# Loading K and Q of two head pairs in one transfer each instead of two

## The chip, the cores and the metric

The kernel runs on one core of a Trainium2 chip. The core has a tensor engine (PE, with its weight loads shown apart as PEld), a vector engine (DVE), a scalar engine (ACT), a general engine (POOL, GpSimd) and a sync engine (SP) that here only starts transfers. Transfers between the chip's memory and the core's on-chip memory are moved by 16 DMA engines that SP, ACT and POOL feed through queues of their own.

The metric is the device time of one execution in microseconds (us); the lower the better. The time before is a median of four runs.

## The reference

Attention over 4 batches, 8 heads, 768 positions and a head size of 64, then a feed-forward layer with a maximum of three products. Some heads ("retrieval") see all earlier positions, the others only the first 4 positions and a window of 64.

```python
scores = (1.0 / np.sqrt(D)) * np.matmul(q, k.transpose(0, 1, 3, 2))
rel = pos[:, None] - pos[None, :]
causal = rel >= 0
stream_keep = causal & ((pos[None, :] < n_sink) | ((rel >= 0) & (rel < window)))
mask = np.where(retr[:, None, None], causal, stream_keep)      # per head
scores = np.where(mask, scores, -1e9)
a = np.exp(scores - max); a = a / (sum(a) + 1e-09)
x = np.matmul(a, v)  ->  (B * S, H * D)                        # 3072 x 512
h = np.maximum(np.maximum(x @ w1, x @ w2), x @ w3)             # 3072 x 768
out = h @ w_out                                                # 3072 x 512
```

## The kernel before

Each batch is cut into two halves of 384 query positions. The unit of attention is a pair of heads (hp 0 to 3), or a group of four heads (a "quad", two pairs). Each pair goes through scores on PE (line 441), exponentials on ACT (line 452), masks, and the product with V on PE (line 495). The feed-forward layer of a half (`ffn`, lines 319 to 373) is cut into small steps that are put between the attention of the next halves, so that PE always has something to do. The order of all work is written out by hand: first a list of calls (lines 539 to 594) for the first half, then a table (lines 602 to 650). Every engine executes its instructions in that order; there is no scheduler that moves them.

The first batch loads K and Q in another way than the later ones. `load_pairs` (line 121) takes a half, the first pair, the number of pairs n and two engines, and starts the transfers of K (on SP for the first half) and of Q (on ACT for the first half) into a staging tile. With its last argument `alone` it starts one transfer per pair; without it, one for all n pairs. Rows of 768 bytes (3 positions of 64 numbers of 4 bytes) are moved. For the first half the calls are: pair 0 (line 213), the flags `ir32` that say which head is of which kind (line 215), pair 1 (line 216), pairs 2 and 3 with `alone` (line 217), and V of the first half in three transfers on SP (`load_v`, line 218). For the second half of the first batch the transfers of pairs 0 and 1 (line 563) and of pairs 2 and 3 (line 579) are started by POOL, one each for K and Q, without `alone`.

Then `cast_pair` (line 135) turns K and Q of a pair into 16-bit numbers: pair 0 on ACT, pair 1's K on POOL and Q on ACT, pairs 2 and 3 on POOL. `turn_pair` (line 147) transposes them on PE (line 157) and copies the result to the tile KQ on DVE (line 162). The order of the calls around this is: cast pair 0; ten matmuls of idle work on PE; flags; turn pair 0; cast pair 1; turn pair 1; cast pair 2; scores of pairs 0 and 1; start of the transfer of w0 on POOL (`load_weight`, line 307); `far_flags` (DVE, and two copies on POOL, line 290); cast pair 3; turn pair 2; scores of pair 1; turn pair 3; the preparation of V (`prep_v`, lines 392 and 394); scores of pairs 2 and 3; products with V. On POOL, casts, starts of transfers and copies stand in one row in this order.

The completion of each transfer that SP or ACT start is told by one of eight semaphores, taken in turn. A transfer that is the ninth to use one waits, on the engine that starts it, until the first has landed. The staging tile of pairs 2 and 3 is one tile for both in either case.

Of the kernel before, what the change touches and what calls it, by code (L numbers as in the profile page):

```python
# [51 lines left out]
def kernel(  # L52
# [14 lines left out]
    nc = tc.nc  # L67
# [53 lines left out]
    def load_pairs(half, hp, n, engines, alone=False):  # L121
        for nm, src, eng in zip(("ks", "qs"), (k, q), engines):
            st = stage.tile([P, 4, HB, D], FP32, tag=nm, name=nm)
            m = 2 if alone else 2 * n
            for h in range(0, 2 * n, m):
                eng.dma_start(
                    out=st[:, h : h + m],
                    in_=src[
                        0, 2 * hp + h : 2 * hp + h + m, half * HALF : (half + 1) * HALF
                    ].rearrange("h (p j) d -> p h j d", p=P),  # L130
                )
            for i in range(n):
                staged.setdefault((half, hp + i), []).append(st[:, 2 * i : 2 * i + 2])
# [69 lines left out]
    def load_v(b, half, engines=None):  # L203
        engines = engines or (nc.sync,) * HB
        vs = stage.tile([P, H, HB, D], FP32, tag="vs", name="vs")
        for j in range(HB):
            r0 = half * HALF + j * P
            engines[j].dma_start(
                out=vs[:, :, j], in_=v[b, :, r0 : r0 + P].rearrange("h p d -> p h d")
            )  # L210
        staged_v[b, half] = vs
# [2 lines left out]
    ir32 = consts.tile([1, 2 * H], mybir.dt.int32, name="ir32")  # L214
    nc.sync.dma_start(out=ir32, in_=is_retrieval.bitcast(mybir.dt.int32).unsqueeze(0))
    load_pairs(0, 1, 1, (nc.sync, nc.scalar))
    load_pairs(0, 2, 2, (nc.sync, nc.scalar), True)
    load_v(0, 0)


# [506 lines left out]
```

## Time and profile before

| what | value |
|---|---|
| median of four runs | 202.36 us (202.06 to 202.9) |
| profiled execution, its time | 202.53 us |
| profiled execution, its span | 200.6 us |
| PE busy | 189.1 us, 94% of the span |
| ACT busy | 131.8 us, 66% |
| DVE busy | 123.7 us, 62% |
| POOL busy | 122.4 us, 61% |
| share of DMA in the chain that ended last | 3% |
| transfers of ks on SP (first half), each | 192 KB, 4 of them |
| transfers of qs on ACT (first half), each | 192 KB, 4 of them |
| transfers of vs on SP, each | 256 KB |

The span goes from the first to the last instruction; the execution's time has 1.9 us more. A timeline row has the start in us, the length, the engine, the line, the operation with output and input, and in brackets how long the engine was idle before and what ended that. The chain that ended last is found by following back from the last instruction what each one waited for. A row of the view of stretches has the stretch, its length, busy time and instructions of PE, PEld, DVE, ACT and POOL, the granted clock of PE, the mean share of the DMA engines and GB/s. The time of a transfer to landing counts from the start of its issue.

### The profile page before, as it was taken

Reading aid. Unit: us, or ns where it says so; the run is one execution under the profiler, and the core shown is the slowest. Engines: PE = TensorE matmul, PEld = TensorE weight load, DVE = VectorE, ACT = ScalarE, POOL = GpSimd, SP = SyncE. Lnnn points to the kernel's source line nnn. Section 1 sums busy time; section 2 is a strip of 40 time slices with the busy share of each in tenths; the row PEclk is TensorE's granted clock in tenths of the full one; section 3 lists DMA queues with packets and bytes.
Section 4 is the critical chain, followed back from the end, with each engine's and each line's share of the span. In section 5 each row is a group of like instructions: output and inputs, shape, how many; then the busy total and the mean of one; then the engine's idle time right before and its main releaser. Section 6 shows DMA issues by size and latency. Waiting matters only on the chain.

```text
span 200.6 us, 5133 instructions
## 1 busy us (share of the span) xinstructions
PE 189.1 (94%) x2059; PEld 109.1 (54%) x2059; DVE 123.7 (62%) x242; ACT 131.8 (66%) x206; POOL 122.4 (61%) x153
## 2 busy tenths in 40 slices
PE   7697999796899999999999999999999999999992
PEld 2355654355566466574655465575655555755652
DVE  2699697999777738871554739961555234443540
ACT  4488698597885777666788595757768769313221
POOL 3499159579987914887969726699937537500000
PEclk9789999999999999999999999999999999999999
DMA  5999999997629993714449998602401220023004
GB/s 182 266 174 276 276 236 211 212 228 178 169 42 165 158 235 133 157 23 116 123 79 147 143 261 139 109 20 75 144 20 23 104 76 20 3 51 147 3 0 157
DMA packets 43245, 26.48 MB, mean 132 GB/s; under 512 B 33558, under 2 KB 38230, under 8 KB 43222
## 3 DMA queue, kind: packets, MB, share of 16 engines
q1 hardware_dynamic: 37206, 15.01, 34.6%
q0 software_dynamic: 4784, 10.23, 26.2%
q10 hardware_dynamic: 1232, 0.92, 1.5%
q8 instruction: 16, 0.26, 0.6%
q14 instruction: 7, 0.06, 0.1%
HBM read 25.17 MB, written 6.29 MB: 157 GB/s over the span
## 4 chain that ended last, share of the span: by engine, by line
PE 82%; ACT 5%; DVE 5%; DMA 3%; issue 2%; SPq 0%; POOL 0%; DVEq 0%; ACTq 0%
PE yy L338 42%; PE yy L364 13%; PE st L441 11%; PE oacc L495 9%; ACT pt L452 3%; PE yst L338 3%; DMA ks<-in_k_dram 2%; DVE KQ L190 2%; PE tr L157 1%; PE st L425 1%; DVE x L505 1%; DMA out_dram<-ot 1%; PE yst L364 1%; ACT va L392 1%; ACT ot L370 1%
## 5 line engine op out<-in xcount | busy, mean ns | idle before, releaser
L479 POOL TENSOR_TENSOR pt<-pt,mk 128x512 f16<-128x512 f16 (+1 forms) x76 | 80.4, 1081 | 37.6 <-ACT pt L452 37.6
L452 ACT ACTIVATE pt<-st 128x1024 f16<-128x1024 f32 (+3 forms) x99 | 83.1, 894 | 22.5 <-PE st L441 21.8
L349 DVE TENSOR_TENSOR acc<-yy,acc 128x384 f16<-128x384 f32 x45 | 25.1, 558 | 27.8 <-PE yy L338 18.4
L338 PE MATMUL yy<-xT,w2t 128*128 128x384 f16 x180 | 35.9, 327 | 1.7 <-DVE hT L349 1.7
L338 PE MATMUL yy<-xT,w1t 128*128 128x384 f16 x180 | 36.1, 327 | 0.1
L338 PE MATMUL yy<-xT,w0t 128*128 128x384 f16 x180 | 35.6, 326 | 0.2 <-DVE xT L531 0.2
L346 ACT CAST acc<-yy 128x384 f16<-128x384 f32 x45 | 21.3, 484 | 17.6 <-PE yy L338 11.2
L364 PE MATMUL yy<-woutt,hT 128*128 128x512 f16 (+1 forms) x138 | 32.0, 375 | 0.0
L441 PE MATMUL st<-KQ 32*128 32x384 f16 (+4 forms) x560 | 29.0, 281 | 0.6 <-DVE KQ L190 0.5
L349 DVE TENSOR_TENSOR hT<-yy,acc 128x384 f16<-128x384 f32 x45 | 24.9, 559 | 6.7 <-PE yy L338 4.3
L495 PEld LDWEIGHTS <-pt 128*128 128x128 f16 x672 | 23.9, 97 | 5.4 <-issue 2.2
L338 PEld LDWEIGHTS <-w2t 128*128 128x128 f16 x192 | 17.6, 98 | 15.2 <-issue 4.0
L190 DVE STREAM_TRANSPOSE KQ<-kq 128x384 f32<-128x384 f32 x24 | 25.7, 1131 | 0.0
L338 PEld LDWEIGHTS <-w0t 128*128 128x128 f16 x192 | 18.2, 98 | 12.7 <-issue 0.8
L495 PE MATMUL oacc<-va,pt 128*128 128x65 f16 x352 | 24.8, 193 | 0.3 <-ACT va L392 0.3
L338 PEld LDWEIGHTS <-w1t 128*128 128x128 f16 x192 | 17.3, 98 | 12.5 <-issue 1.3
L370 ACT COPY ot<-yy 128x512 f32<-128x512 f32 x22 | 12.9, 588 | 15.5 <-PE yy L364 9.3
L495 PE MATMUL oacc<-vf,pt 128*128 128x65 f16 x320 | 21.1, 193 | 0.9 <-POOL vf L394 0.9
L364 PEld LDWEIGHTS <-hT 128*128 128x128 f16 x150 | 13.9, 98 | 14.6 <-issue 0.3
L441 PEld LDWEIGHTS <-KQ 32*128 32x128 f16 (+1 forms) x560 | 12.2, 93 | 17.7 <-issue 12.4
L505 DVE TENSOR_TENSOR x<-oacc,rc 128x384 f16<-128x384 f32 x32 | 17.8, 558 | 1.3 <-DVE rc L503 0.3
L503 DVE RECIPROCAL rc<-oacc 128x6 f32<-128x6 f32 x32 | 6.2, 192 | 20.2 <-PE oacc L495 19.8
(71 smaller groups left out, 129.5 us busy)
## 6 DMA issues: line engine op xcount, KB each, us to landing
out_dram<-ot SPq DMA_DIRECT2D x23, 256.0 KB, 3.1
vs<-in_v_dram SPq DMA_DIRECT2D x21, 256.0 KB, 6.3
kq<-in_k_dram POOLq DMA_DIRECT2D x6, 384.0 KB, 5.8
kq<-in_q_dram POOLq DMA_DIRECT2D x6, 384.0 KB, 8.1
qs<-in_q_dram ACTq DMA_DIRECT2D x4, 192.0 KB, 4.4
ks<-in_k_dram SPq DMA_DIRECT2D x4, 192.0 KB, 4.4
w0t<-in_moe_w_dram POOLq DMA_DIRECT2D x1, 768.0 KB, 7.0
ks<-in_k_dram POOLq DMA_DIRECT2D x2, 384.0 KB, 6.8
```

What stands on the lines that cost most here:

```text
L190: nc.vector.transpose(out=dst.rearrange("c (p j) -> c j p", j=n)[:, j0:j1], in_=src.rearrange("c (j i) -> c j i", i=R),)
L338: nc.tensor.matmul(yy[:, 0:HALF], w_t[wi][:, ks, ni * P : (ni + 1) * P], xT[b, half][ks].rearrange("p a t -> p (a t)"), start=(ks == 0), s ...
L346: nc.scalar.copy(out=acc[ni], in_=yy[:, 0:HALF])
L349: nc.vector.tensor_tensor(out=dst, in0=yy[:, 0:HALF], in1=acc[ni], op=ALU.max)
L364: nc.tensor.matmul(yo[:, 0:n], hT[ns][:, tb * P : (tb + 1) * P], woutt[:, ns, c : c + n], start=(ns == 0), stop=(ns == NNB - 1),)
L370: op(out=ot[:, c : c + n], in_=yo[:, 0:n])
L441: nc.tensor.matmul(sts[g // m][:, g % m, c0 : c0 + n * P], KQ[rows, 0, ki * P : (ki + 1) * P], KQ[rows, 1, t0 : t0 + n * P], start=(c0 == ...
L452: nc.scalar.activation(out=pts[t, i][:, u, h0 : h0 + m, 0:w], in_=st[:, :, 0:w], func=AF.Exp, scale=sc,)
L479: engine.tensor_tensor(out=x, in0=x, in1=m, op=ALU.mult)
L495: nc.tensor.matmul(o[:, qi, hl, 0 : D + 1], pt[:, u, hl, c : c + P], vv[:, 2 * hp + hl, ki, 0 : D + 1], start=(idx == 0), stop=(idx == len ...
L503: nc.vector.reciprocal(out=rc, in_=o[:, :, :, D])
L505: nc.vector.tensor_tensor(out=x, in0=o[:, :, :, 0:D], in1=rc.unsqueeze(3).to_broadcast([P, HB, 2, D]), op=ALU.mult,)
```

## The change

K and Q of pairs 2 and 3 of the first half are loaded by one transfer of 384 KB each, where there were two of 192 KB each. Nothing else is edited. The staging tile, the rows moved and the casts are the same; each cast of pair 2 or 3 now reads from a transfer that carries both pairs. There are two transfers fewer among those that take the eight semaphores in turn, so each later one takes a semaphore two places on. In the second half the loads were already one transfer each.

```diff
     load_pairs(0, 1, 1, (nc.sync, nc.scalar))
-    load_pairs(0, 2, 2, (nc.sync, nc.scalar), True)
+    load_pairs(0, 2, 2, (nc.sync, nc.scalar))
     load_v(0, 0)
```

## The prediction

> **What bounds the kernel now.** Read in this order: the page's busy shares, its chain of work, the order of events in the first 20 us on PoolE, the tensor engine's clock by window, and the DMA issues with their landings. PE is busy for 94% of the span and the chain belongs to it; DMA holds 3%, so a load counts only where it is on the chain.
>
> ```profile
> PE 189.1 (94%) x2059; PEld 109.1 (54%) x2059; DVE 123.7 (62%) x242; ACT 131.8 (66%) x206; POOL 122.4 (61%) x153
> PE 82%; ACT 5%; DVE 5%; DMA 3%; issue 2%; SPq 0%; POOL 0%; DVEq 0%; ACTq 0%
> ```
>
> The change is in the first microseconds, so the chain in order of time is read there. It goes from K of pair 1 (landed 6.71) over one PoolE cast to PE, and PE is without a gap from 7.32 to 13.2, where ACT's exponentials take over:
>
> ```profile
> 1.71 5.00 DMA ks<-in_k_dram
> ...
> 6.76 0.51 POOL kn L139
> ...
> 7.32 0.53 PE tr L157 x6
> ...
> 12.07 0.44 PE tr L157 x6
> 12.51 0.33 PE st L425 x4
> 12.84 0.34 PE st L441 x4
> ...
> 13.20 1.35 ACT pt L452 x3
> ```
>
> PE works strictly in order here, so a late input of the transposes at 12.07 (pair 3) holds all that follows. Those inputs come from PoolE, whose timeline is (start, length, instruction, idle before it and what ended it):
>
> ```profile
> 7.97 0.51 POOL L139 CAST kn<-ks 128x384 f16<-128x384 f32 x1 [0.70 <-DMA ks<-in_k_dram]
> 8.42 0.51 POOL L139 CAST qn<-qs 128x384 f16<-128x384 f32 x1
> 8.87 0.93 POOL L307 DMA_DIRECT2D w0t<-in_moe_w_dram  x1
> 9.99 0.71 POOL L290 COPY vf<-far 128x32 f16<-128x32 f16 x2 [0.19 <-PE st L441]
> 10.53 0.68 POOL L139 CAST kn<-ks 128x384 f16<-128x384 f32 x1
> 11.15 0.56 POOL L139 CAST qn<-qs 128x384 f16<-128x384 f32 x1
> ```
>
> PoolE waits 0.70 us for pair 2's K and after that only 0.19 us before it has cast pair 3's Q (end 11.71). The last view gives, per stretch, PE's busy time, its granted clock (third from the end of the line) and DMA:
>
> ```profile
> 4.27:7.68 3.41, 1.70 (x18) 0.97 (x17) 1.32 (x5) 1.84 (x5) 0.50 (x1) 1.00 1.10 312
> 7.68:11.10 3.42, 3.42 (x23) 1.36 (x20) 3.16 (x9) 1.57 (x3) 2.95 (x6) 0.50 1.26 194
> 14.51:17.92 3.41, 2.77 (x61) 2.19 (x59) 3.10 (x10) 2.56 (x5) 3.41 (x6) 1.00 1.09 307
> ```
>
> A stretch with PE half idle (1.70 of 3.41) is followed by one at half clock; one with 2.77 of 3.41 is not (17.92 to 21.34 ran at 1.00). DMA is saturated (share about 1) from 3 us on.
>
> Landings, issue plus time to landing: pair 0 K 4.0, Q 4.3; pair 1 Q 5.0, K 6.71 (15 of its 16 completions were in by 5.45, one came late); pair 2 Q 6.95, K 2.15+5.8 = 7.92; pair 3 Q 8.14, K 4.29+4.4 = 8.67; V 9.87, 11.01, 11.98. So transfers land nearly in the order of issue, some 0.6 us apart.
>
> [...]
>
> **The change, part by part.**
>
> 1. *Removed: two issues.* SP issues ks three times instead of four, ACT qs three instead of four. ACT saves one issue, 0.50 us (the issues at 1.34, 1.87 and 2.39 are about 0.52 apart), so its table load starts near 2.4, not 2.91, and the cast of pair 0's K can begin at its landing, 4.05, not 4.31. Gain: nothing, because PE runs its warm-up matmuls until 5.06 and transposes pair 0 at 5.10; those casts were done at 4.80 and 5.22. Without that cover it would be 0.26 us.
>
> 2. *Removed: SP's wait.* SP sat 1.7 us before the fourth ks (issued 4.29, after pair 0's Q had landed), because eight completion counters go round among transfers of SP and ACT and that one was the ninth. With two transfers fewer, the merged ks (2.15) and the first V (about 2.6) go without a wait, the second V follows at 4.29, the third at about 4.9. In the kernel before V went at 4.70, 5.22, 5.84. Earlier issue gains nothing in landings: [...] the same bytes stand in the same order in front of V. SP's next instruction after V is at 35.92, so a V issue [...] (the third took 2.48 us before) holds nobody.
>
> 3. *Added: pair 2 waits for pair 3.* Casts of pair 2's K and Q on PoolE now need the whole merged transfers. I expect Q to land between 7.0 and 8.2 and K, last, at L. The bytes up to that point are the same 1.57 MB as before, so L should be that of the old last piece, 8.67; [...] so I take 8.75. Bounds: 7.92, if it is as early as pair 2's K alone was, and 9.1, if one engine is late by as much again as the spread within ks of pair 3 (about 0.4).
>
> 4. *What PoolE does with it.* Cast K at L+0.05, cast Q 0.45 later, issue of w0 0.45 later for 0.93: free at L+1.88 (before: 9.80). The vf copies start at the later of 9.99 (they need the far flags) and L+1.88: a shift of L−8.11, for 8.75 0.64 us; 0.19 us of the 0.83 is absorbed there. The rest follows without a gap: pair 3's K cast at 11.17 to 11.85, its Q cast 11.79 to 12.35.
>
> 5. *What PE does.* Hand-over PoolE to PE took 0.06 (7.26 to 7.32). Pair 2's transposes at 11.12 need its Q cast, over at 9.76: covered. Pair 3's K, needed at 12.00, is there at 11.91. Pair 3's Q, needed at 12.12 by the weight load, is there at 12.41: a stall of 0.29 us. In general the stall is L−8.46, nothing below that. Queued behind it on PE are the masks and scores of pairs 2 and 3; ACT, which already waited 0.39 us at 13.20, waits 0.29 more, and its exponentials, the V cast at 15.70 and the output matmuls at 16.14 are on the chain. After that the chain is compute of PE, ACT and DVE to the last store, so I pass the 0.29 on in full.
>
> 6. *PoolE's own later issues* (K, Q of the second half at 12.03, w1, w2, V) move by up to 0.64, and w0 by 0.83. Cover: w0 landed at 15.89 and is read at 18.46; second-half Q landed 18.25 and its ACT cast is at 18.72; w1 22.66 against 23.52; w2 28.61 against 29.96; V of the second half 32.11 against an ACT cast that could start at 32.82. The tightest are 0.47 and 0.71, plus the 0.29 that the readers move too; the DMA engines are full of V until 11 to 12 us, so the landings move by less than the issue, some 0.4. Cost nothing; if that cover is gone, the excess over 0.7.
>
> Sum: 0 + 0 + 0.29 + 0 = +0.29 us on the profiled execution: span 200.6 to 200.9, time 202.53 to 202.82. The median of the four runs, 202.36, is 0.17 under that execution; since part 5 sets an absolute time for pair 3's Q, whatever PE did before, I keep 202.82, 0.46 over the median (0.2%).
>
> **Rivals.**
>
> *Hidden.* L is 8.46 or less [...]: PoolE's slack and PE's place at 12.12 take it all. For it: 0.39 us of the 0.83 us is absorbed anyway. Against it: the bytes are the same and the engines were at their limit. Time 202.4 to 202.5.
>
> *Faster.* The late engine of pair 1's K (6.71 against 5.45) was an accident of when V was being issued, and goes away. PE then starts up to 0.7 us earlier, perhaps without the half-clock stretch, but still meets pair 3's Q. With L = 7.92 and the far flags earlier by as much, that is there at L+3.66 = 11.58 instead of 12.12: 0.54 us gained, 202.0; at L = 7.6, 0.86 us, 201.7. It decides only below an L of 8.4, which I think unlikely.
>
> *Much slower: a second half-clock stretch.* If pair 3's stall and the waits after it bring PE's busy time in one 3.41 us window towards the 1.70 that was followed by half clock, the next one runs at half. Price: the window 14.51 to 17.92 holds 2.77 us of PE work; at half clock it does 1.71 of them, so at most 1.06 are left over, and at least the 0.54 that the chain itself spends on PE's output matmuls at 16.14; I take 0.8: 203.6. It decides where idle time in a window rises by between 0 and 1.07 us over the 0.64 that was harmless; [...].
>
> *Pair 1's K later,* because V is now being issued while it moves: each 0.1 us goes straight into the chain at 6.76, but shows only in so far as PE comes to 12.12 later than pair 3's Q, 12.41: the first 0.29 is free. With pair 1's K at 7.3 (0.6 late): 202.53+0.6 = 203.1.
>
> **How the numbers follow.** Stall as reckoned 0.48 (own range 202.55 to 203.2), hidden 0.18, half clock or late pair 1 0.20 (203.0 to 203.6), faster 0.14 (201.4 to 202.1). The measurement of this kernel can tell about 0.3%, 0.6 us, from no change: below 201.75 is faster, above 202.97 slower. Of the main case I put 0.22 over 202.97 (L over 8.9) and 0.26 under it, of the faster case 0.08 under 201.75. Slower 0.22+0.20 = 0.42; same 0.26+0.18+0.06 = 0.50; faster 0.08. Range 202.2 to 203.5: about a tenth lies below it, a tenth above.
>
> **What would show it.** In the changed kernel's profile: PoolE's first two waits for ks at 6.8 and about 8.8; w0 issued near 9.65; the gap before the vf copies gone; a wait of PE on PoolE's casts near 12.1 to 12.4 that was not there; V landing at about 10, 11, 12 as before; SP without the 1.7 us wait. I am wrong if ks lands before 8.4, if K of pair 1 lands at another time than 6.7, if a half-clock stretch appears or vanishes, or if ACT at 13.2 moves and the end does not.

## The result, and the profile after

| kernel | median, us | runs | range, us |
|---|---|---|---|
| before | 202.22 | 53 | 201.21 to 203.18 |
| changed | 203.41 | 32 | 201.92 to 205.08 |

Time changed to before: 1.0056, with a 95% interval of 1.0043 to 1.0068. The changed kernel is slower by 0.56%, some 1.1 us, where 0.3% can be told from no change. The forecast was 202.8 (0.2% to 0.3% slower), range 202.2 to 203.5: the time lies near the upper end of the range, and on the other side of the line between "no change" and "slower" from the likeliest case. The ratio leaves out four executions of the changed kernel, those more than 1.5% above its fastest. The execution profiled for the changed kernel took 204.96 us, 1.55 more than the median, with PE at half clock from 11.57 to 18.40, so I show beside it the same kernel profiled again (e5), an execution of 204.0 us at full clock.

Busy times and the shares of the chain, from the page of the changed kernel:

```profile
PE 191.0 (94%) x2059; PEld 109.9 (54%) x2059; DVE 123.0 (61%) x242; ACT 132.2 (65%) x206; POOL 122.0 (60%) x153
PE 81%; DVE 5%; issue 4%; ACT 3%; DMA 3%; POOL 1%; SPq 0%; DVEq 0%; ACTq 0%; POOLq 0%
```

and from the page of the changed kernel profiled again:

```profile
PE 188.9 (93%) x2059; PEld 109.0 (54%) x2059; DVE 123.3 (61%) x242; ACT 131.9 (65%) x206; POOL 121.9 (60%) x153
PE 74%; DMA 10%; POOL 5%; DVE 4%; ACT 2%; issue 2%; SPq 0%; DVEq 0%; ACTq 0%
```

The work is that of before. In the second page the chain has moved: DMA has 10% of it where it had 3%, and PoolE 5% where it had nothing. What PoolE does at the place of the change is read from its timeline, first in the changed kernel (columns as in the prediction's view):

```profile
9.38 0.68 POOL L139 CAST kn<-ks 128x384 f16<-128x384 f32 x1 [3.20 <-DMA ks<-in_k_dram]
10.01 0.56 POOL L139 CAST qn<-qs 128x384 f16<-128x384 f32 x1
10.51 0.93 POOL L307 DMA_DIRECT2D w0t<-in_moe_w_dram  x1
```

and then, with pair 3's casts and the next issue, in the repeated profile:

```profile
9.68 0.56 POOL L139 CAST kn<-ks 128x384 f16<-128x384 f32 x1 [2.37 <-DMA ks<-in_k_dram]
10.18 0.56 POOL L139 CAST qn<-qs 128x384 f16<-128x384 f32 x1
10.69 0.93 POOL L307 DMA_DIRECT2D w0t<-in_moe_w_dram  x1
11.62 0.48 POOL L290 COPY vf<-far 128x32 f16<-128x32 f16 x2
11.92 0.51 POOL L139 CAST kn<-ks 128x384 f16<-128x384 f32 x1
12.37 0.50 POOL L139 CAST qn<-qs 128x384 f16<-128x384 f32 x1
...
13.19 0.81 POOL L126 DMA_DIRECT2D ks<-in_k_dram  x1
```

Pair 2's K cast starts at 9.38 and 9.68, where it started at 7.97. PoolE stood idle for it 3.20 and 2.37 us, where it was 0.70. w0 goes out at 10.51 and 10.69 (8.87 before), and from there the row has no gap, so K of the second half is issued at 13.19 where it was 12.03. On PE this shows as a wait that was not there. PE's timeline of the repeated profile, pair 3's K and Q:

```profile
12.48 0.34 PE L157 MATMUL tr<-ident,kn 128*128 128x128 f16 x3 [0.91 <-POOL kn L139]
12.93 0.34 PE L157 MATMUL tr<-ident,qn 128*128 128x128 f16 x3
```

Pair 3's Q is transposed at 12.93, 0.75 us after the 12.18 of before, whose line is

```profile
12.18 0.33 PE L157 MATMUL tr<-ident,qn 128*128 128x128 f16 x3
```

The clock of PE in the stretches of the profile first shown (columns as in the prediction's view):

```profile
8.16:11.57 3.41, 2.29 (x20) 1.05 (x20) 2.56 (x10) 2.44 (x5) 2.19 (x4) 1.00 0.81 152
11.57:14.98 3.41, 2.67 (x18) 1.33 (x18) 2.08 (x4) 1.02 (x3) 3.41 (x8) 0.50 0.85 123
14.98:18.40 3.42, 3.42 (x33) 1.85 (x34) 1.72 (x5) 2.73 (x6) 3.42 (x6) 0.50 1.12 292
```

Two stretches at half clock (0.50) follow one in which PE was busy for 2.29 of 3.41 us. In the repeated profile the clock was 1.00 throughout.

### The profile page after: what moved, and what is told of

Its sections match the earlier page's. It is cut to its first block, busy times and chain, and to the rows that moved or that the text cites. A ratio compares the mean times of both kernels' runs of the same rounds, so it can differ in the third digit from the quotient of the medians.

```text
span 203.0 us, 5132 instructions
## 1 busy us (share of the span) xinstructions
PE 191.0 (94%) x2059; PEld 109.9 (54%) x2059; DVE 123.0 (61%) x242; ACT 132.2 (65%) x206; POOL 122.0 (60%) x153
## 4 chain that ended last, share of the span: by engine, by line
PE 81%; DVE 5%; issue 4%; ACT 3%; DMA 3%; POOL 1%; SPq 0%; DVEq 0%; ACTq 0%; POOLq 0%
PE yy L338 42%; PE yy L364 13%; PE st L441 11%; PE oacc L495 10%; PE yst L338 3%; ACT pt L452 2%; DVE KQ L190 2%; DMA ks<-in_k_dram 2%; DVE x L505 1%; PE tr L157 1%; PE st L425 1%; DMA out_dram<-ot 1%; PE yst L364 1%; ACT ot L370 1%; POOL kn L139 0%
```

## The experiments

My theory was that of the prediction: pair 2's K lands with the last packet of a transfer twice as long, PoolE's row starts later by that, and PE waits for pair 3's Q. The rivals: that V, issued 2 us earlier, gets in the way; that the lost or new half-clock stretches make the difference; and that the row of loads behind PoolE's casts carries the loss, not pair 3. Each run stands against the kernel before on the same chip (medians 202.0 to 202.25).

**The change again (e5).**

> The changed kernel once more, for a profile at full clock. Theory 1 (pair 2's casts wait for the whole of K, and PoolE, being in order, carries the lateness to pair 3's casts and to PE): 203.2 to 203.5 us, about 1.1 over the kernel before; K of pairs 2 and 3 lands between 8.4 and 9.3, PoolE casts pair 2's K right after it, and PE waits on PoolE ahead of the transposes of pair 3 for 0.5 us or more. Theory 2 (V, issued earlier, takes the engines' time from K and Q): K of pair 1 lands later than 6.7 and PE first waits longer than 1.7 us there. Theory 3 (half clock): the granted clock shows a half-speed stretch in every run that is over 203.

Measured: 203.97 us, 1.0084 (1.0056 to 1.0112). Slower again, and by more than the 203.2 to 203.5 that I expected; K landed at 9.62, later than the 9.3 of that text. The intervals of the two comparisons, 0.43 to 0.68% and 0.56 to 1.12%, only overlap. Part of the difference goes with the clock. A stretch of 3.41 us at half clock takes about 0.008 off the mean granted clock of an execution of 200 us (3.41 × 0.5 / 200); the profile before, with one, has 0.991. Four of the nine executions have a mean of 0.992 and took 203.80 to 204.80 us; the other five have 0.997 or more, with a median of 203.43, and four of these took over 203 us. So theory 3, a half-clock stretch in every run over 203, is wrong.

**K alone, Q alone (e1, e2).** e1 merges K only and leaves Q in two transfers; e2, the second diff, merges Q only:

```diff
-            m = 2 if alone else 2 * n
+            m = 2 if alone and nm == "qs" else 2 * n
```

> K of pairs 2 and 3 in one transfer, Q still in two. Theory 1: PoolE's cast of pair 2's K is the first to wait, and it waits for the whole of K as in the changed kernel, so nearly the whole loss is here: +0.8 to +1.1 us over the kernel before. Theory 2: half of the shift of V's issue, +0.5. If Q's transfer were what is late: 0.

```diff
-            m = 2 if alone else 2 * n
+            m = 2 if alone and nm == "ks" else 2 * n
```

> Q of pairs 2 and 3 in one transfer, K still in two. Theory 1: pair 2's K lands near 7.9 as before and its cast ends near 8.4; Q of both pairs lands near 8.0 to 8.2, ahead of that: within 0.3 us of the kernel before. Theory 2: half of the shift of V's issue, +0.5. If Q's transfer were what is late: +0.8 to +1.1.

Measured: e1 203.82 us, 1.0104 (1.0064 to 1.0144); e2 202.76 us, 1.0027 (1.0011 to 1.0044). PoolE's timeline, pair 2's K cast in e1:

```profile
9.03 0.52 POOL L139 CAST kn<-ks 128x384 f16<-128x384 f32 x1 [2.43 <-DMA ks<-in_k_dram]
```

and the same cast with the issue of w0 in e2:

```profile
7.89 0.51 POOL L139 CAST kn<-ks 128x384 f16<-128x384 f32 x1 [1.16 <-DMA ks<-in_k_dram]
...
8.95 0.94 POOL L307 DMA_DIRECT2D w0t<-in_moe_w_dram  x1
```

With K merged the cast is late by 1.06 us (9.03 against 7.97); with Q merged it is where it was, and w0 goes out at 8.95 (8.87 before). Most of the loss is the merged K's. Neither size is what theory 1 gave. e1 loses about 2.1 us, where 0.8 to 1.1 was expected; three of its six executions have a mean clock of 0.992 or less, and the other three took 203.48 to 203.81. e2 loses about 0.55 us, where at most 0.3 was expected. That is the figure of theory 2, but in e2 the first V was issued only 0.27 us earlier (4.43 against 4.70). I can't place this loss: in e2's profile the first w1 of the table below is 0.17 us late behind the second half's Q, and no run shows a link from Q's transfer to that.

**No merge, only the order (e3).** The two transfers of each stay, but pair 3's goes first:

```diff
-            for h in range(0, 2 * n, m):
+            for h in reversed(range(0, 2 * n, m)):
```

> Transfers as before, one a pair, but pair 3's K and Q are issued ahead of pair 2's: nothing is merged, the number of transfers and V's place are as before, only pair 2 lands last. Theory 1: pair 2's K lands near 8.7, the loss of the merge without a merge: +0.7 to +1.1 us over the kernel before. Theory 2 and any cost of the size of a transfer: 0, as the kernel before.

Measured: 203.24 us, 1.0061 (1.0032 to 1.0091). Number and size of the transfers are those of before, V is issued as before, and the loss is that of the change. PoolE's timeline in e3:

```profile
9.56 0.57 POOL L139 CAST kn<-ks 128x384 f16<-128x384 f32 x1 [1.62 <-DMA ks<-in_k_dram]
```

w0 went out at 10.59. Both times are near those of the changed kernel (9.38 and 10.51). So what costs is that pair 2's K comes last. (This one profiled execution took 204.37 us, 1.13 over its median; pair 1's K was late in it too, cast at 7.44 and not at 6.76, and PE had a half-clock stretch from 8.59 to 12.01.)

**V back in its place (e4).** The changed kernel with two loads of 64 bytes, which nothing uses, ahead of V on SP. In the profiles before and after, the ninth transfer that SP and ACT issue waits until pair 0's Q has landed (the fourth ks at 4.29, the second V at 4.33); here the second of the two loads is to be the ninth and to hold V back. V's own issue in e4 was not measured:

```diff
+    for i in range(2):
+        filler = consts.tile([1, 2 * H], mybir.dt.int32, name=f"filler{i}")
+        nc.sync.dma_start(
+            out=filler, in_=is_retrieval.bitcast(mybir.dt.int32).unsqueeze(0)
+        )
```

> The changed kernel with two tiny transfers (64 bytes, a second and third copy of the head flags that nobody reads) put between the merged K and V on SP, so that V is again held back as in the kernel before (issued from about 4.7 on). Theory 1 (pair 2 waits for the whole of K): still +0.6 to +0.9% over the kernel before. Theory 2 (the earlier V is what slows K, and adds to the landing of the merged K): K of pairs 2 and 3 lands near 8.7 instead of 9.3 to 9.6, +0.3% or less.

Measured: 203.58 us, 1.0055 (1.0026 to 1.0084). The loss stays, and PoolE's wait with it:

```profile
9.42 0.66 POOL L139 CAST kn<-ks 128x384 f16<-128x384 f32 x1 [3.31 <-DMA ks<-in_k_dram]
```

If V was held back as planned, its earlier issue is not the cause of the loss: it is 0.55% as against 0.56%. (The profiled execution, 205.23 us, was the longest of the eight.)

**No half clock in the kernel before (e9).** Five matmuls whose results aren't used fill PE while it waits for pair 1's K:

```diff
+    idle_work(5)
```

> The kernel before with five matmuls on zeros (no result used) between pair 0's and pair 1's transposes, where PE waits for pair 1's K. Theory 3 (the half-clock stretch after that wait costs time): it goes, PE reaches pair 3 earlier, but pair 3's Q cast (11.7) and ACT's exponentials set the pace: 0 to 0.4 us gained. If PE's clock there were on the path in full: 1 to 1.7 us gained.

Measured: 202.34 us, 1.0007 (0.9995 to 1.0019). These medians can't say what the stretch costs, because it is rare: all 22 executions of e9, and all 29 of the kernel before on that chip, have a mean clock of 0.996 or more. Of the 90 executions of the kernel before in all these comparisons only two have less, 0.992; they took 202.84 and 203.02 us. So the profile that the prediction was worked out from, with a mean of 0.991, shows an uncommon execution. What the stretch hid there is seen in e9's profile, where K of pairs 1 and 2 was cast no earlier (6.88 and 8.08). PE's timeline at pair 3:

```profile
11.37 0.34 PE L157 MATMUL tr<-ident,kn 128*128 128x128 f16 x3 [0.18 <-ACT pt L452]
11.88 0.34 PE L157 MATMUL tr<-ident,qn 128*128 128x128 f16 x3 [0.17 <-POOL qn L139]
```

At full clock PE is there earlier, pair 3's Q goes 0.30 us earlier, at 11.88 and not 12.18, and PE already waits for PoolE's cast of it, as it does in the profiles of e2 and e7 (0.17 and 0.16 us).

The rival, that half clock makes the loss, is answered by the executions without a stretch. Of the changed kernel, 33 executions have their clock on record (one more than the table counts). 26 have a mean of 0.998 or more, and their median is 203.29; the medians of the kernel before without its two executions at 0.992 are 202.0 to 202.25. So a loss of about 1.1 us stands at full clock. The other seven took 203.86 to 205.08 us. Such executions are more frequent after the change (7 of 33, and 4 of 9 in e5) than before it (2 of 90). Whether the stretch makes them longer or comes of the waits that do isn't shown; the same filling in the changed kernel wasn't tried.

**w0 moved later (e6, e7).** In e6 in the changed kernel, in e7 in the kernel before, the issue of w0 goes behind pair 3's casts, so that pair 3 doesn't stand behind it:

```diff
-    load_weight(0)
...
     cast_pair(0, 3, (pool, pool))
+    load_weight(0)
```

> The changed kernel with PoolE's issue of w0 (0.93 us) moved from ahead of pair 3's casts to behind them. Theory 1 says that PoolE's row carries the lateness: pair 3's Q cast ends 0.9 us earlier, PE's wait of 0.9 us ahead of pair 3 goes, and 0.6 to 0.9 us of the loss come back: +0.1 to +0.4% over the kernel before. If the loss went another way (V, Q of the second half): no gain, +0.6 to +0.9%, or more, because w0 and all behind it on PoolE land later.

> The same move of w0's issue in the kernel before, as the control. Theory 1: pair 3's casts were ready about when PE came to them, so 0 to 0.3 us gained; with w0 and the second half's Q landing up to 0.9 us later, 0 to 0.6 us lost: between -0.15% and +0.3%.

Measured: e6 204.83 us, 1.0132 (1.0102 to 1.0162); e7 204.78 us, 1.0137 (1.0102 to 1.0172). Both are slower than the change, and alike; theory 1 gave at most 0.4% and 0.3%. In e7 nothing is merged, and PE's timeline shows why:

```profile
19.27 2.77 PE L338 MATMUL yy<-xT,w0t 128*128 128x384 f16 x16 [1.36 <-DMA w0t<-in_moe_w_dram]
```

ACT waits 2.77 us at 20.49 for the second half's K. w0 issued 2.5 us later (11.38 against 8.87) arrives after PE wants it, and the loads behind it land later too (that K at 20.41, where it was 17.06). That a step behind pair 2's casts can cost a per cent by its own lateness is shown here without any merge.

**w0 moved earlier (e10, e11, e13).** If its lateness were the whole loss, w0 ahead of pair 2's casts should give it back:

```diff
+    load_weight(0)
     cast_pair(0, 2, (pool, pool))
...
-    load_weight(0)
```

> The kernel before with PoolE's issue of w0 moved ahead of pair 2's casts, so that it doesn't wait for pair 2's K. Theory A (what counts in the lateness of pair 2 is that w0's issue stands behind it on PoolE, and with w0 the whole row of later loads, whose Q of the second half ACT waits for): w0 is issued near 7.3 instead of 8.9, the second half's Q lands earlier, 0.3 to 0.8 us gained on the kernel before. Theory B (what counts is PE's wait for pair 3's casts): 0 to 0.3 us gained, as pair 3's casts are hardly earlier.

> The same move in the changed kernel. Theory A: w0 no longer waits for the merged K, and the loss of the merge goes, also because 0.93 us of PoolE's row behind the merged K is gone: within 0.2% of the same move in the split kernel, so at or under the kernel before. If the loss is made elsewhere (V's place, the size of a transfer): still 0.5% or more over the split kernel with the same move.

Measured: e10 (before) 205.32 us, 1.0133 (1.0097 to 1.0169); e11 (changed) 204.37 us, 1.0121 (1.0083 to 1.0160). DVE's timeline of e10, at the preparation of V:

```profile
17.07 1.19 DVE L392 CAST va<-vs 128x384 f16<-128x384 f32 x2 [4.24 <-DMA vs<-in_v_dram]
```

w0, issued at 5.99, moves beside V's three transfers (10.3 us from issue to landing, 7.0 in the kernel before), and the cast of V that began at 13.42 in the kernel before begins at 17.07. In e11 PE waits 2.56 us behind the same cast. The gain that was expected of the earlier w0 did not come in either. e13 put w0 in between in the changed kernel, near the time at which the kernel before issues it, with five fills of an unused tile as a spacer:

```diff
+    busy = consts.tile([P, 256], FP16, name="busy")
+    for _ in range(5):
+        nc.gpsimd.memset(busy, 0.0)
+    load_weight(0)
     cast_pair(0, 2, (pool, pool))
...
-    load_weight(0)
```

> The changed kernel with w0's issue on PoolE ahead of pair 2's casts, and five fills of an unused tile (some 1.9 us, result not used) ahead of it, so that w0 is issued between 8 and 9.2 us as in the kernel before and not at 6.0, where it collided with V. Pair 2's K stays merged and as late as before (8.5 to 9.6), pair 3's casts follow it without 0.93 us of issue between. If the loss of the merge is the lateness of PoolE's row behind pair 2's K (w0's issue, pair 3's casts): within 0.25% of the kernel before. If the lateness of pair 2 itself (PE waits for its transposes near 10 us) or V's place counts: +0.4 to +0.7%.

Measured: 204.35 us, 1.0113 (1.0078 to 1.0148). PE waits 1.57 us at 17.47 behind the cast of V. w0 went at 7.74, a microsecond earlier than in the kernel before, and V was late again. The run was to divide the loss between pair 3 and the loads behind w0, and it doesn't. In both pairs (e6 and e7, e10 and e11) the merge makes no difference beyond the intervals, but all four meet another, larger wait, which can hide it. Half-clock stretches, too, are more frequent in these five runs (19 of 27 executions have a mean clock of 0.992 or less).

**PoolE later by hand (e12).** The kernel before, with three fills of an unused tile (1.18 us) ahead of pair 3's casts and behind the issue of w0:

```diff
+    busy = consts.tile([P, 256], FP16, name="busy")
+    for _ in range(3):
+        nc.gpsimd.memset(busy, 0.0)
     cast_pair(0, 3, (pool, pool))
```

> The kernel before with three fills of an unused tile on PoolE (some 0.9 us) between w0's issue with the copies behind it and pair 3's casts: pair 3's casts are as late as in the changed kernel, w0 is on time. Theory B: PE waits at pair 3 until about 12.9, +0.6 to +0.9 us over the kernel before. Theory A: ACT, which waits for the second half's Q later on anyway in part of the runs, gives most of it back: 0 to +0.4 us.

Measured: 203.56 us, 1.0055 (1.0032 to 1.0078). A later row on PoolE costs what the change costs, though nothing is merged and w0 isn't behind the fills; all eleven executions have a mean clock of 0.995 or more. Its profiled execution doesn't show the way well: pair 2's K had come early (cast at 6.87), PE waited 0.88 us for the cast of pair 3's K, and pair 3's Q was transposed at 11.96, near the 11.88 of e9. The time was lost later, at the second weight:

```profile
24.02 0.82 PE L338 MATMUL yy<-xT,w1t 128*128 128x384 f16 x4 [0.39 <-DMA w1t<-in_moe_w_dram]
```

w1 had been issued only 0.18 us later than before (14.74 against 14.56) and landed 1.32 us later (23.98 against 22.66), so it isn't shown that the fills made it late.

**Where the time is lost, over the profiled executions.** The timelines of PE and ACT give five times for each (us; "run of w0" is the start of the row of 14 matmuls with w0, "Q cast" ACT's first cast of Q of the second half, "first w1" the first matmul with w1, the last column the execution's time less "first w1"):

| kernel | pair 2's K cast | pair 3's Q on PE | run of w0 | Q cast | first w1 | time | rest |
|---|---|---|---|---|---|---|---|
| before | 7.97 | 12.18 | 19.17 | 18.72 | 23.52 | 202.53 | 179.0 |
| e9 | 8.08 | 11.88 | 19.04 | 19.76 | 23.58 | 202.62 | 179.0 |
| e2 | 7.89 | 11.63 | 18.80 | 19.87 | 23.69 | 202.77 | 179.1 |
| e12 | 6.87 | 11.96 | 19.12 | 18.87 | 24.02 | 203.24 | 179.2 |
| e1 | 9.03 | 12.19 | 19.69 | 20.75 | 24.57 | 203.65 | 179.1 |
| e5 | 9.68 | 12.93 | 20.09 | 21.47 | 25.29 | 204.00 | 178.7 |
| e3 | 9.56 | 13.03 | 21.03 | 20.35 | 25.38 | 204.37 | 179.0 |
| changed | 9.38 | 12.75 | 21.89 | 21.48 | 26.24 | 204.96 | 178.7 |

The rest is 178.7 to 179.2 in all, and in the six profiled executions that the table leaves out: what an execution gains or loses is settled when the first matmul with w1 starts, some 25 us in, and passes to the end. That start follows three limits, and the latest rules. It comes 4.35 us after the run of w0 (before 23.52 − 19.17, e3 and changed the same), or 3.82 after the Q cast (e9, e2, e1 and e5, to the hundredth), or when w1 has landed (e12). For e5 this divides its 1.77 us: the run of w0 is later by 0.92, which is the 0.75 of pair 3 and 0.17 on the way through DVE; it would give 24.44. The Q cast gives 25.29, another 0.85. In e1 pair 3 is no later than in the profile before, the run of w0 is by 0.52 (PE waits 0.37 of it, at 13.23, for DVE's copy of the transposed tiles), and the Q cast adds 0.53. Against e9, which had no half-clock stretch, pair 3 is later by 0.31 in e1 and by 1.05 in e5. This division is a reading of single executions, not an experiment on the medians.

## Why the prediction was right in its range and not in all its steps

*Part 1 (ACT's issue)* was right. The table load starts at 2.39 and the cast of pair 0's K at 4.05, both as worked out, and nothing came of it.

*Part 2 (SP's wait)* was right in the issues: V starts at 2.67, and the 1.7 us wait is gone. The second V, now the ninth, goes at 4.33 (I had 4.29) after a wait of 1.1 us for pair 0's Q, the third at 4.74, and its issue keeps SP for 4.2 us, which holds nobody, as I had said: SP's next transfer starts at 38.64. Its landings were wrong: 10.68, 11.79 and 12.75 in the repeated profile, 0.8 later than before. In e4, which was built to hold V back again, the loss is as large, so it seems not to hang on that.

*Part 3 (when the merged K lands)* named the right mechanism with the wrong size. I took L = 8.75, at most 9.1, both estimates from the landings of before. The DMA issues of the changed kernel say, after the size, the time from issue to landing:

```profile
qs<-in_q_dram ACTq DMA_DIRECT2D x1, 384.0 KB, 6.2
ks<-in_k_dram SPq DMA_DIRECT2D x1, 384.0 KB, 7.2
```

K was issued at 2.16, so L = 9.32; it was 9.62 in e5. In the changed kernel 15 of the 16 completions were in at 8.34, and the last came a microsecond later. The cast of pair 2's K, which reads half of that transfer, began at 9.38, after the sixteenth; that of pair 1's K before began at 6.76, also after the sixteenth (6.71) and not after the fifteenth (5.45). So I had seen such a late completion (that it is one engine's is my reading; the trace tells only the times), and for my bound took the spread of another transfer, 0.4. Casts of pair 2's K began at 6.87 to 8.08 in the split kernels of the table that keep the order, and at 9.03 to 9.68 in those that merge K.

*Parts 4 and 5 (PoolE and pair 3)*: the formula for the stall, L − 8.46, gives 0.86 us for L = 9.32, and 202.53 + 0.86 = 203.39, the measured median to 0.02. That is partly luck. With L = 9.62 it gives 1.16 and e5's trace shows 0.75: PoolE's copies took 0.48, not 0.71, and pair 3's casts 0.51 and 0.50, not 0.68 and 0.56, so pair 3's Q was cast 3.25 us after L and not 3.60. What is missing came from elsewhere. The constant was one execution's too: 8.46 rests on PE coming to pair 3's Q at 12.12, and PE came so late because it ran at half clock from 7.68. At full clock (e9) it already waits for PoolE there, so the 0.54 us of slack between an L of 7.92 and 8.46 isn't there in the usual execution. (The rival *Hidden* gives what is absorbed as 0.39 us of the 0.83; by the sums of parts 4 and 5 it is 0.54.)

*Part 6 (PoolE's later issues cost nothing)* is the step that failed. I put the shift of the landings at 0.4 us, on the ground that the engines were full of V. In e5 the second half's K is issued 1.16 later, w0 lands 17.66 (15.89 before), and Q 21.39 (18.25). ACT's timeline:

```profile
21.47 0.51 ACT L139 CAST qn<-qs 128x384 f16<-128x384 f32 x1 [1.89 <-DMA qs<-in_q_dram]
```

In the profile before, without a wait:

```profile
18.72 0.51 ACT L139 CAST qn<-qs 128x384 f16<-128x384 f32 x1
```

Two things make Q's landing that late. Its fifteenth completion, which leaves out one late one, was in at 18.22 before and at 19.32, 19.76 and 20.0 in e1, the first profile of the changed kernel and e5: later by 1.10, 1.54 and 1.78 us. w0, the first in PoolE's row of loads, was issued later by 1.08, 1.64 and 1.82. So the lateness passed to the landings nearly in full, where I had put 0.4. The sixteenth completion came 0.03 us after the fifteenth before, and 1.4 us after it in e5.

PE stands behind ACT's cast: ACT clears PE's results away after it (from 22.72 on in e5), and PE waits 0.61 us for that:

```profile
23.23 0.33 PE L157 MATMUL tr<-ident,kn 128*128 128x128 f16 x3 [0.61 <-ACT acc L346]
```

My cover of 0.47 us was read from one execution in which Q took 5.4 us from issue to landing. In e9, with the loads of before, it took 6.7, in e2 7.1, and in e1 and e5 7.4; in e9 ACT already waited 1.23 us for it, and the first w1 moved by only 0.06. So the cover is used up without the change whenever Q is that slow, and a later issue passes through. The chain of the repeated profile, in order of time, goes along this row and never through pair 3's scores:

```profile
10.18 0.56 POOL qn L139
10.74 0.88 POOL w0t L307
...
13.23 0.58 POOL ks L126
...
14.00 0.83 POOL qs L126
...
20.55 13.74 DMA vs<-in_v_dram
```

It ends in the second half's V, landed at 34.29 (32.11 before) for an ACT cast at 34.59 (32.82): the 0.71 of cover that I had counted there has shrunk to 0.30. This is not a further loss, since the first w1 was late by the same 1.77 already; V had time to spare, so the way of this chain is a hint and no proof.

*The rivals.* Hidden did not happen: L was above 8.46 in every profiled execution with K merged. Faster did not: pair 1's K came early in the changed kernel's first profile (5.59) and as before in the second (6.75), and in both PE then waited 0.91 us for pair 3's K. Nor was pair 1's K late. Two of the signs that I had named for being wrong did appear: that 5.59, and the half-clock stretch of before, which is gone in the second profile. The half clock did come in the first profile, for two stretches where I had priced one at 0.8 us: from pair 3's Q to the run of w0 took 9.14 us, against 7.16 in e5. Part of that 2.0 covers the wait for Q, so that the first w1 is later by only 0.95 than in e5. My reading of what brings such a stretch was wrong as well. From e5's windows:

```profile
4.74:8.15 3.41, 1.89 (x22) 1.15 (x22) 1.56 (x6) 1.13 (x3) 0.50 (x1) 1.00 1.08 285
8.15:11.57 3.42, 2.99 (x27) 1.34 (x26) 3.37 (x10) 2.60 (x4) 1.90 (x3) 1.00 0.86 166
```

Busy for 1.89 of 3.41 us and full clock after; in the changed kernel's first profile 2.29 and half clock after. The busy share of a stretch in this view doesn't decide it. The loss of the median doesn't need that case: it stands in the executions at full clock (203.29 against 202.0 to 202.25).

*What stays open*: how the loss of the median divides between pair 3's casts and the loads behind them. The runs made to divide it (e6, e11, e13) each ran into another wait. The traces say about half each in e5; no experiment says it. Open too are the 0.27% of e2 and what brings a half-clock stretch.

## What to carry to other kernels

Here the first consumer of two joined loads waited for all of both: the cast of pair 2's K began at 9.38 and 9.68, where it began at 7.97. Where the consumers take the pieces one after another on an engine that also issues later loads, look at the first consumer's time and at everything queued behind it, the issues of loads too, down to the readers of those loads. Cover read from one profiled execution is one draw of a landing time that spread over 2 us here (5.4 to 7.4 us for Q of the second half); take the longest landing that any trace shows for that size before an edit is costed at nothing. A slack that stands beside a half-clock stretch may be gone in an execution without it (0.54 us by the sums for the profile before; in e9 PE already waits 0.17 us there); the mean clock of the other executions tells how common the stretch is.

## What the runs showed of the hardware

- The last of a transfer's 16 completions can lag far behind the fifteenth: 6.71 against 5.45 for pair 1's K before, 9.32 against 8.34 for the merged K, 21.39 against 20.0 (e5) and 19.79 against 18.18 (e2) for Q of the second half. It isn't so in each execution: pair 1's K was cast at 5.4 to 5.6 in e6, e7, e10 and e11. Once there, the lag stayed much the same in the next transfers of PoolE's queue: 1.6, 1.6, 1.6 and 1.5 us from Q on in e2 (Q, w1, K, Q), 0.8 to 0.9 from w1 on before.
- The time at which a large load is issued can be wrong on both sides. w0 at 8.87 keeps nobody waiting; at 11.38 PE waits 1.36 us for it, and at 5.99 DVE waits 4.24 us for V, whose transfers run beside it.
- Shortly ahead of the late landing of the second half's Q, the trace has a packet of 16 KB of the instruction queue that takes 1.1 to 1.2 us (17.40 in e2, 18.61 in e5). That it delays the last completion is a guess; no run tested it, and in the profile before the same packet (17.22) stands ahead of a Q whose last completion was not late (0.03 us after the fifteenth).
